# Two tokens of Q and K in a partition, transposed on VectorE as 4-byte pairs

## The chip, the cores and the metric

The kernel runs on one core of one Trainium2 chip. The time is that of the device for one execution, in microseconds (us). Three executions of the kernel before took 408.53, 409.21 and 410.55 us; the median, 409.21, is the time before.

## The reference

Inputs are Q, K and V of shape 8 x 8 x 576 x 64 (batch, head, token, width) and four weight matrices, all fp32. Sliding-window attention comes first: each token attends to itself and the 63 tokens before it.

```
scores = q @ k.T / sqrt(64)
scores = where(0 <= pos_q - pos_k < 64, scores, -1e9)
attn   = exp(scores - max) / (sum + 1e-9)
x      = attn @ v                # heads side by side: 4608 tokens x 512
out    = ((x @ w1) * (x @ w2)) @ w3 @ w_out      # 512 -> 1024 -> 1024 -> 512
```

The output is 4608 x 512 in fp32.

## The kernel before

The kernel works in fp16 with fp32 sums. At the start it folds w3 and w_out into one matrix (`fold_t`, `fold_mm`), so the second half of the network is two matrix products, `ffn_ab` (line 374) and `ffn_o` (line 392).

**Loads.** `load_qk` brings Q or K of one batch into a tile of 128 partitions with two DMAs from GpSimd's queue, which also convert to fp16. A partition holds 18 consecutive tokens of one head, for each of two heads: partition 32 j + p holds tokens 18 p to 18 p + 17 of heads 2 j and 2 j + 1. Each DMA moves one head of each pair as one contiguous piece of 2304 bytes (in SBUF) for each partition. `load_v` brings V in blocks of 128 tokens, in pieces of 128 bytes.

**Transposition.** `transposes(b, which, hh)` is one VectorE instruction (line 211) for one head of each pair. It transposes blocks of 32 x 32 elements inside each group of 32 partitions, so that the 64 components of a head lie on 32 partitions, in two halves c = 0 and c = 1. The tile is ordered (half, token). Blocks are read as 32 consecutive elements; on the write side the fastest index is p, the partition of origin, and tokens p and p + 1 of one block lie 18 elements apart. There are four such instructions for each batch: K and Q, each for hh = 0 and 1.

**Scores.** `scores(n)` takes one of three segments of a batch. It issues 32 matmuls (line 249) with 32 contracted rows, four groups of partitions side by side, and adds the halves c = 0 and c = 1. `weigh` applies the exponential on ScalarE (line 259) and two masks on GpSimd (lines 267 and 269).

**Values.** `values(d)` multiplies probabilities with V (line 312; line 296 in the first two batches), takes the logarithm of the sums and an exponential on ScalarE, and VectorE multiplies (lines 321 and 322, or 304) into the ring `xT`. `ffn_ab` then ends with a VectorE product (line 380) and `ffn_o` with a VectorE copy (line 394) and a store by the SP queue.

**Order.** The order is written out by hand (`manual_schedule`). The first two batches (`SHORT = 2`) are straight-line code. From tick 24 on a batch is twelve ticks, and a list of FFN pieces with due times calls `tick(u)` between them. `late` says which extra steps a tick r of a batch issues, with the batch they are for:

```
late = {0: [("load", 2, "k")], 1: [("t", 1, "k", 0), ("load", 2, "q")], 2: [("v", 1, 0, 2)],
        3: [("t", 1, "q", 0), ("v", 1, 3)], 5: [("t", 1, "k", 1), ("v", 1, 4, 5)], 7: [("t", 1, "q", 1)],
        8: [("copy", 1, 4)], 9: [("copy", 1, 1)]}
```

So K of batch b + 2 is loaded at tick 0 of batch b, and the transpositions of batch b + 1 stand at ticks 1, 3, 5 and 7. Each engine works through its own queue in this order. Score tiles and value tiles come from one pool with two buffers (`ps_a`); FFN tiles from another with four (`ps_f`). The tiles of loaded Q and K have two buffers each.

Of the kernel before, what the change touches and what calls it, by code (L numbers as in the profile page):

```python
# [9 lines left out]
FP16 = mybir.dt.float16  # L10
I32 = mybir.dt.int32
# [4 lines left out]
P = 128  # L16
# [128 lines left out]
def kernel(  # L145
# [11 lines left out]
    nc = tc.nc  # L157
    B, H, S, D = q.shape
# [4 lines left out]
    NJ = H // 2  # L163
    TI = 18
# [5 lines left out]
    SHORT = 2  # L170
# [11 lines left out]
    sb = fast.enter_context(tc.tile_pool(name="sb", bufs=2))  # L182
# [13 lines left out]

    t16s, kTs, qTs = {}, {}, {}

    def load_qk(b, which):
        src = k if which == "k" else q  # L200
        t = sb.tile([P, 2, TI * D], FP16, name=which + "16", bufs=2)
        for hh in range(2):
            nc.gpsimd.dma_start(out=t[:, hh], in_=src[b, hh:H:2].rearrange("j (p r) d -> j p (r d)", r=TI))
        t16s[which, b] = t

    def transposes(b, which, hh):

        dst = kTs if which == "k" else qTs
        if hh == 0:
            dst[b] = sb.tile([P, 2, 2, S], FP16, name=which + "T")  # L210
        nc.vector.transpose(dst[b][:, hh].rearrange("q c (p i) -> q i c p", i=TI), t16s[which, b][:, hh].rearrange(  # L211
            "p (i c e) -> p i c e", c=2, e=32))

    def v_heads(b):
        return v16s[b % 2].rearrange("p c j (a e) -> p c (j a) e", a=2)[:, :, :, 0:D]
# [19 lines left out]
    def scores(n):  # L235

        b, si = divmod(n, 3)
        kT, qT = kTs[b], qTs[b]
        seg = SEGS[si]
        w = sum(blk[2] for blk in seg)  # L240
        s_ps = [ps_a.tile([P, 2, 512], FP32, name="a_ps") for _ in range(2)]
        c0 = 0
        for (k0, q0, m, _) in seg:
            for a in range(2):
                for c in range(2):
                    for j in range(NJ):
                        part = slice(32 * j, 32 * j + 32)
                        o0 = 256 * a + c0
                        nc.tensor.matmul(s_ps[j // 2][:, j % 2, o0:o0 + m], kT[part, a, c, k0:k0 + P],  # L249
                                         qT[part, a, c, q0:q0 + m], start=(c == 0), stop=(c == 1),  # L250
                                         skip_group_check=True)
            c0 += m
        for jp in range(2):
            weigh(2 * n + jp, s_ps[jp].rearrange("k j (a n) -> k j a n", a=2)[:, :, :, 0:w], si, w)

    def weigh(d, s_ps, si, w):

        pt = sb.tile([P, 2, 2, 256], FP16, name="pt", bufs=6)
        nc.scalar.activation(pt[:, :, :, 0:w], s_ps, AF.Exp, bias=-SHIFT, scale=scale)  # L259

        rows = pt.rearrange("k j a n -> k (j a) n")
        for (lo, nb, n, off, step) in MASKS[si]:
            sl = rows[:, :, lo:lo + nb * n]
            pat = [[0, 4], [step, nb], [1, n]]
            if nb == 1:
                pat = [[0, 4], [1, n]]
            nc.gpsimd.affine_select(out=sl, in_=sl, pattern=pat, compare_op=ALU.is_ge,  # L267
                                    fill=0.0, base=off, channel_multiplier=-1)
            nc.gpsimd.affine_select(out=sl, in_=sl, pattern=[[-s, m] for s, m in pat], compare_op=ALU.is_ge,  # L269
                                    fill=0.0, base=63 - off, channel_multiplier=1)  # L270
        probs[d] = pt
# [62 lines left out]
    def event(b, kind, ahead, *a):  # L334
        if b + ahead >= B:
            return
        do = {"load": load_qk, "t": transposes, "v": load_v, "copy": copy_v}[kind]
        do(b + ahead, *a)
# [3 lines left out]
    def tick(u):  # L342

        b, r = divmod(u, 12)
        n, m = divmod(u, 4)
        if m == 0 and n < NS:
            scores(n)
        if m in (1, 2) and 6 < n <= NS:
            values(2 * n - 3 + m)
        for e in late.get(r, []):  # L350
            event(b, *e)
        if m == 3 and 6 < n <= NS:
            keep_sums(n - 1)
# [4 lines left out]
    def ffn_ab(g, fc, nf=1, lo=0, hi=GT):  # L358

        if g not in abs_:  # L360
            abs_[g] = sb.tile([P, 8, GT], FP16, name="ab", bufs=3)
        ab = abs_[g]
        n = hi - lo
        a_ps = ps_f.tile([P, GT], FP32, name="f_ps")
        b_ps = ps_f.tile([P, GT], FP32, name="f_ps")
        x0 = (g * GT + lo) % RING
        cuts = [(0, n)] if x0 + n <= RING else [(0, RING - x0), (RING - x0, n)]
        for w, d in ((w1_sb, a_ps), (w2_sb, b_ps)):
            first = True
            for f in range(nf):  # L370
                for dc in range(4):
                    for c0, c1 in cuts:
                        xc = (x0 + c0) % RING
                        nc.tensor.matmul(d[:, f * n + c0:f * n + c1], w[:, dc, (fc + f) * P:(fc + f + 1) * P],  # L374
                                         xT[:, dc, xc:xc + c1 - c0], start=first, stop=(dc == 3),
                                         skip_group_check=True)
                        first = False
        a_sb = sb.tile([P, GT], FP32, name="a_sb", bufs=3)
        act_cp(a_sb[:, 0:nf * n], a_ps[:, 0:nf * n])  # L379
        nc.vector.tensor_tensor(ab[:, fc:fc + nf, lo:hi], b_ps[:, 0:nf * n].rearrange("p (f n) -> p f n", f=nf),  # L380
                                a_sb[:, 0:nf * n].rearrange("p (f n) -> p f n", f=nf), ALU.mult)
# [92 lines left out]
    def fold_step(fc):  # L474
        if fc + 1 < 8:
            w3Ts[fc + 1] = fold_t(fc + 1)
        fold_mm(fc, w3Ts.pop(fc), act_cp if fc % 4 == 3 else dve_cp)

    load_qk(0, "k")
    load_qk(0, "q")  # L480
    load_wo()
    load_w3(0)
# [3 lines left out]
    for hh in range(2):  # L486
        transposes(0, "k", hh)
        transposes(0, "q", hh)
    keep_busy(30)
    load_v(0, 0, 2, 3)  # L490
    load_w3(2)
    load_w3(3)
    scores(0)
    keep_busy(15)
    scores(1)
    keep_busy(15)
    w3Ts[0] = fold_t(0)
# [69 lines left out]
    for g in range(1, NG):  # L567
        part = [lambda g=g, fc=fc: ffn_ab(g, fc) for fc in range(8)] + \
# [60 lines left out]
```

## Time and profile before

| | |
|---|---|
| median of three runs | 409.21 us (408.53 to 410.55) |
| the profiled execution | 407.49 us |
| its span | 405.8 us |
| TensorE busy, mean granted clock | 291.7 us, 0.852 |
| VectorE busy | 300.1 us |
| ScalarE busy | 149.7 us |
| GpSimd busy | 169.0 us |
| packets on DMA queue 0 (GpSimd's) | 58640 |

The profile is one execution on the chip. In it PE is TensorE, DVE is VectorE, ACT is ScalarE, POOL is GpSimd, SP is the engine that issues the stores; L211 is line 211 of the kernel. The granted clock is the share of full speed that TensorE was given: 1.00 is 2.4 GHz, 0.50 is 1.2 GHz. The span begins with the first recorded instruction and ends with the last; the execution's own time is 1.7 us longer.

### The profile page before, as it was taken

The numbers are of one execution on the slowest core, as the hardware profiler recorded it, in microseconds if no ns is written. First come the engines' busy times: TensorE is split into PE (matmuls) and PEld (weight loads), VectorE is DVE, ScalarE is ACT, GpSimd is POOL, SyncE is SP. The second block draws the span as 40 slices with busy tenths as digits, with TensorE's granted clock in tenths as the row PEclk, the third lists the DMA queues.
The fourth block names the chain that finished last, engine by engine and source line by source line (L and its number), as shares of the span: only waits on it lengthen the run. The fifth ranks groups of instructions, "written<-read, shape, count | busy, mean of one in ns | idle before, by whom it ended". The sixth has DMA issues, their size and how long they took to land.

```text
span 405.8 us, 6273 instructions
## 1 busy us (share of the span) xinstructions
PE 291.7 (72%) x2474; PEld 153.8 (38%) x2474; DVE 300.1 (74%) x267; ACT 149.7 (37%) x256; POOL 169.0 (42%) x218
## 2 busy tenths in 40 slices
PE   8008895747067454987679567978696779999995
PEld 8006452223033212443234233855342335455442
DVE  2892756976956399779977997598969896655542
ACT  1003162125023602364426433524464337764220
POOL 6307943118046852186127704535424533540300
PEclk9757999569668855996889887989899789999999
DMA  5990499911409990129312980299206410020203
GB/s 61 203 188 17 40 165 160 144 15 32 48 28 104 121 128 0 54 69 138 22 52 62 133 38 27 80 124 52 80 28 39 46 55 29 26 80 1 106 1 107
DMA packets 64097, 29.47 MB, mean 73 GB/s; under 512 B 51088, under 2 KB 54416, under 8 KB 64064
## 3 DMA queue, kind: packets, MB, share of 16 engines
q0 software_dynamic: 58640, 19.45, 51.3%
q1 hardware_dynamic: 5280, 9.46, 6.6%
q8 instruction: 20, 0.33, 0.4%
q14 instruction: 13, 0.11, 0.1%
q10 hardware_dynamic: 144, 0.13, 0.1%
HBM read 38.80 MB, written 9.44 MB: 119 GB/s over the span
## 4 chain that ended last, share of the span: by engine, by line
PE 40%; DVE 26%; issue 16%; DMA 10%; POOL 6%; ACT 1%; DVEq 0%; POOLq 0%
PE f_ps L374 22%; PE f_ps L392 11%; DVE qT L211 10%; DVE kT L211 9%; DMA k<-in_k_dram 7%; PE a_ps L312 4%; DMA q<-in_q_dram 3%; DVE ab L380 3%; PE a_ps L249 2%; POOL pt L269 2%; POOL pt L267 2%; DVE xT L322 2%; DVE xT L321 1%; DVE t2k L394 1%; POOL v L223 1%
## 5 line engine op out<-in xcount | busy, mean ns | idle before, releaser
L374 PE MATMUL f_ps<-xT,w_sb 128*128 128x512 f16 (+1 forms) x640 | 151.5, 392 | 30.1 <-DVE ab L380 23.8
L267 POOL TENSOR_SCALAR_AFFINE_SELECT pt<-pt 128x512 f16<-128x512 f16 (+1 forms) x64 | 52.0, 813 | 169.8 <-ACT pt L259 169.8
L374 PEld LDWEIGHTS <-w_sb 128*128 128x128 f16 x640 | 64.3, 104 | 99.3 <-issue 52.4
L211 DVE STREAM_TRANSPOSE kT<-k 128x1152 f16<-128x1152 f16 x16 | 81.9, 5119 | 16.4 <-DMA k<-in_k_dram 16.1
L259 ACT ACTIVATE pt<-a_ps 128x1024 f16<-128x1024 f32 (+1 forms) x48 | 43.1, 950 | 118.3 <-PE a_ps L249 118.3
L211 DVE STREAM_TRANSPOSE qT<-q 128x1152 f16<-128x1152 f16 x16 | 82.1, 5134 | 0.1
L392 PE MATMUL f_ps<-wc_sb,ab 128*128 128x512 f16 (+1 forms) x296 | 75.9, 411 | 7.6 <-DVE ab L380 7.6
L380 DVE TENSOR_TENSOR ab<-f_ps,a_sb 128x512 f16<-128x512 f32 x72 | 51.4, 723 | 32.9 <-PE f_ps L374 18.4
L379 ACT COPY a_sb<-f_ps 128x512 f32<-128x512 f32 x72 | 41.8, 581 | 62.6 <-PE f_ps L374 62.6
L249 PE MATMUL a_ps<-qT,kT 32*128 32x128 f16 (+1 forms) x768 | 19.2, 234 | 63.2 <-DVE xT L322 29.0
L269 POOL TENSOR_SCALAR_AFFINE_SELECT pt<-pt 128x512 f16<-128x512 f16 (+1 forms) x64 | 51.9, 811 | 4.4
L392 PEld LDWEIGHTS <-ab 128*128 128x128 f16 x296 | 29.7, 105 | 44.3 <-issue 10.3
L223 POOL DMA_DIRECT2D v<-in_v_dram x40 | 34.1, 856 | 19.5 <-DMA k<-in_k_dram 17.4
L249 PEld LDWEIGHTS <-kT 32*128 32x128 f16 x768 | 13.7, 103 | 74.4 <-issue 44.2
L394 DVE COPY t2k<-f_ps 128x512 f32<-128x512 f32 (+1 forms) x36 | 24.8, 693 | 13.1 <-PE f_ps L392 12.4
L321 DVE TENSOR_TENSOR xT<-a_ps,r 64x384 f16<-64x384 f32 x36 | 19.6, 546 | 19.0 <-ACT r L320 19.0
L318 ACT ACTIVATE ln_s<-a_ps 64x384 f32<-64x384 f32 x36 | 17.5, 487 | 40.1 <-PE a_ps L312 40.0
L312 PEld LDWEIGHTS <-v 128*128 128x128 f16 x288 | 20.4, 106 | 9.2 <-issue 3.2
L312 PE MATMUL a_ps<-pt,v 128*128 128x128 f16 (+1 forms) x288 | 23.0, 229 | 0.0
L322 DVE TENSOR_TENSOR xT<-a_ps,r 64x384 f16<-64x384 f32 x36 | 20.2, 561 | 0.5
L320 ACT ACTIVATE r<-ln_s 128x384 f32<-128x384 f32 x36 | 18.8, 523 | 1.1
L319 ACT ACTIVATE ln_s<-a_ps 64x384 f32<-64x384 f32 x36 | 17.4, 482 | 0.4
(41 smaller groups left out, 147.5 us busy)
## 6 DMA issues: line engine op xcount, KB each, us to landing
out_dram<-t2k SPq DMA_DIRECT2D x35, 256.0 KB
k<-in_k_dram POOLq DMA_DIRECT2D x16, 288.0 KB, 11.4
q<-in_q_dram POOLq DMA_DIRECT2D x16, 288.0 KB, 12.1
v<-in_v_dram POOLq DMA_DIRECT2D x32, 128.0 KB, 11.1
w_sb<-in_moe_w_dram POOLq DMA_DIRECT2D x4, 512.0 KB, 12.2
ab<-in_moe_w_out_dram POOLq DMA_DIRECT2D x1, 1024.0 KB, 15.7
ab<-in_moe_w_dram POOLq DMA_DIRECT2D x2, 512.0 KB, 18.2
xT<-in_moe_w_dram POOLq DMA_DIRECT2D x2, 512.0 KB, 14.7
```

What stands on the lines that cost most here:

```text
L211: nc.vector.transpose(dst[b][:, hh].rearrange("q c (p i) -> q i c p", i=TI), t16s[which, b][:, hh].rearrange("p (i c e) -> p i c e", c=2, ...
L223: nc.gpsimd.dma_start(out=vh[lo:P, c], in_=v[b, :, s0:s0 + P - lo, :].rearrange("h s d -> s h d"))
L249: nc.tensor.matmul(s_ps[j // 2][:, j % 2, o0:o0 + m], kT[part, a, c, k0:k0 + P], qT[part, a, c, q0:q0 + m], start=(c == 0), stop=(c == 1), ...
L259: nc.scalar.activation(pt[:, :, :, 0:w], s_ps, AF.Exp, bias=-SHIFT, scale=scale)
L267: nc.gpsimd.affine_select(out=sl, in_=sl, pattern=pat, compare_op=ALU.is_ge, fill=0.0, base=off, channel_multiplier=-1)
L269: nc.gpsimd.affine_select(out=sl, in_=sl, pattern=[[-s, m] for s, m in pat], compare_op=ALU.is_ge, fill=0.0, base=63 - off, channel_multip ...
L312: nc.tensor.matmul(o_ps[:, jj, o0:o0 + n], v16[:, si * 2 + bi, j0 + jj, a * D:a * D + P], pt[:, jj, a, c0:c0 + n], start=first, stop=(bi = ...
L374: nc.tensor.matmul(d[:, f * n + c0:f * n + c1], w[:, dc, (fc + f) * P:(fc + f + 1) * P], xT[:, dc, xc:xc + c1 - c0], start=first, stop=(dc ...
L379: act_cp(a_sb[:, 0:nf * n], a_ps[:, 0:nf * n])
L380: nc.vector.tensor_tensor(ab[:, fc:fc + nf, lo:hi], b_ps[:, 0:nf * n].rearrange("p (f n) -> p f n", f=nf), a_sb[:, 0:nf * n].rearrange("p ...
L392: nc.tensor.matmul(o_ps[:, 0:c1 - c0], ab[:, fc, t * P:t * P + P], wc_sb[:, fc, c0:c1], start=(fc == 0), stop=(fc == 7))
L394: cp(o_sb[:, c0:c1], o_ps[:, 0:c1 - c0])
```

## The change

A partition holds runs of r consecutive tokens instead of 18: runs of nine in batches 0 and 1, runs of two in batches 2 to 7. A run of two has nine repeats in a partition, a run of nine has two. `load_qk` issues one DMA for each pair of heads (32 partitions, both heads) instead of one for each member of the pairs (128 partitions): four DMAs instead of two, with pieces of 1152 bytes in SBUF (r = 9) or 256 bytes (r = 2).

`transposes` views two neighbouring fp16 components as one 4-byte integer, so an instruction moves 576 elements instead of 1152. The transposed tile is ordered (token, parity): components 2 e and 2 e + 1 of a token lie side by side on partition e, and tokens p and p + 1 of a block lie r elements of 4 bytes apart. The score matmuls contract the even components and then the odd ones (c is now the parity), and read K and Q with a step of two fp16 elements. Nothing else is changed.

```diff
+    def run(b):
+        return 9 if b < SHORT else 2
+
     def load_qk(b, which):
         src = k if which == "k" else q
+        r = run(b)
         t = sb.tile([P, 2, TI * D], FP16, name=which + "16", bufs=2)
-        for hh in range(2):
-            nc.gpsimd.dma_start(out=t[:, hh], in_=src[b, hh:H:2].rearrange("j (p r) d -> j p (r d)", r=TI))
+        for j in range(NJ):
+            nc.gpsimd.dma_start(
+                out=t[32 * j:32 * j + 32].rearrange("p hh (i n) -> p (hh i) n", n=r * D),
+                in_=src[b, 2 * j:2 * j + 2].rearrange("hh (i p r) d -> p (hh i) (r d)", p=32, r=r))
         t16s[which, b] = t
 
     def transposes(b, which, hh):
         dst = kTs if which == "k" else qTs
+        r = run(b)
         if hh == 0:
-            dst[b] = sb.tile([P, 2, 2, S], FP16, name=which + "T")
-        nc.vector.transpose(dst[b][:, hh].rearrange("q c (p i) -> q i c p", i=TI), t16s[which, b][:, hh].rearrange(
-            "p (i c e) -> p i c e", c=2, e=32))
+            dst[b] = sb.tile([P, 2, S, 2], FP16, name=which + "T")
+        nc.vector.transpose(
+            dst[b][:, hh].rearrange("q t c -> q (t c)").bitcast(I32).rearrange("q (i p r) -> q i r p", p=32, r=r),
+            t16s[which, b][:, hh].bitcast(I32).rearrange("p (i r e) -> p i r e", r=r, e=32))
...
-                        nc.tensor.matmul(s_ps[j // 2][:, j % 2, o0:o0 + m], kT[part, a, c, k0:k0 + P],
-                                         qT[part, a, c, q0:q0 + m], start=(c == 0), stop=(c == 1),
+                        nc.tensor.matmul(s_ps[j // 2][:, j % 2, o0:o0 + m], kT[part, a, k0:k0 + P, c],
+                                         qT[part, a, q0:q0 + m, c], start=(c == 0), stop=(c == 1),
```

## Rows read from the trace of the kernel before

**Rows 1.** The page, busy us (share of the span) and instructions of each engine.

```profile
PE 291.7 (72%) x2474; PEld 153.8 (38%) x2474; DVE 300.1 (74%) x267; ACT 149.7 (37%) x256; POOL 169.0 (42%) x218
```

**Rows 2.** The page, the chain that ended last: shares by line.

```profile
PE f_ps L374 22%; PE f_ps L392 11%; DVE qT L211 10%; DVE kT L211 9%; DMA k<-in_k_dram 7%; PE a_ps L312 4%; DMA q<-in_q_dram 3%; DVE ab L380 3%; PE a_ps L249 2%; POOL pt L269 2%; POOL pt L267 2%; DVE xT L322 2%; DVE xT L321 1%; DVE t2k L394 1%; POOL v L223 1%
```

**Rows 3.** Groups by line and shape: busy us, mean ns | idle before.

```profile
L211 DVE STREAM_TRANSPOSE qT<-q 128x1152 f16<-128x1152 f16 x16 | 82.1, 5134 | 0.1
L211 DVE STREAM_TRANSPOSE kT<-k 128x1152 f16<-128x1152 f16 x16 | 81.9, 5119 | 16.4 <-DMA k<-in_k_dram 16.1
L380 DVE TENSOR_TENSOR ab<-f_ps,a_sb 128x512 f16<-128x512 f32 x72 | 51.4, 723 | 32.9 <-PE f_ps L374 18.4 <-ACT a_sb L379 13.6
...
L223 POOL DMA_DIRECT2D v<-in_v_dram x40 | 34.1, 856 | 19.5 <-DMA k<-in_k_dram 17.4 <-DMA w_sb<-in_moe_w_dram 2.0
...
L394 DVE COPY t2k<-f_ps 128x512 f32<-128x512 f32 x35 | 24.3, 700 | 12.1 <-PE f_ps L392 11.4
...
L203 POOL DMA_DIRECT2D k<-in_k_dram x16 | 11.6, 727 | 1.0 <-issue 0.8
```

**Rows 4.** Windows: length, busy us of each engine, granted clock, DMA share, GB/s.

```profile
65.90:87.60 21.70, 9.54 (x34) 3.12 (x33) 21.70 (x8) 1.80 (x4) 5.20 (x7) 0.68 1.37 120
87.60:125.00 37.40, 19.11 (x232) 9.67 (x232) 27.83 (x20) 12.42 (x20) 18.11 (x23) 0.77 0.26 35
125.00:144.30 19.30, 11.60 (x116) 5.18 (x116) 9.01 (x11) 9.03 (x15) 13.78 (x21) 0.77 0.99 128
144.30:163.00 18.70, 11.39 (x56) 4.15 (x56) 18.58 (x10) 3.02 (x4) 6.67 (x8) 0.51 1.16 49
163.00:350.00 187.00, 147.57 (x1226) 78.04 (x1225) 157.07 (x150) 86.64 (x152) 81.07 (x105) 0.89 0.48 61
350.00:405.80 55.80, 50.86 (x311) 24.92 (x308) 26.81 (x43) 21.36 (x39) 12.33 (x11) 0.99 0.16 58
```

**Rows 5.** Windows, VectorE's busy time with line 211 alone.

```profile
144.30:163.00 18.70, 15.20 (x3) 0.51 1.16 49
163.00:350.00 187.00, 81.97 (x16) 0.89 0.48 61
```

**Rows 6.** The chain that ended last, in order of time: start us, us, what.

```profile
1.61 9.65 DMA k<-in_k_dram
...
31.20 0.66 PE a_ps L249 x21
...
213.98 0.45 PE a_ps L249 x32
...
219.47 1.20 DVE kT L211
```

**Rows 7.** Timeline of VectorE: start us, us, what [idle before, releaser].

```profile
65.90 5.10 DVE L211 STREAM_TRANSPOSE kT<-k 128x1152 f16<-128x1152 f16 x1 [2.37 <-DMA k<-in_k_dram]
...
177.76 5.12 DVE L211 STREAM_TRANSPOSE kT<-k 128x1152 f16<-128x1152 f16 x1
```

**Rows 8.** Timeline of TensorE, near 185 us.

```profile
184.69 1.03 PE L249 MATMUL a_ps<-qT,kT 32*128 32x128 f16 x30 [3.91 <-DVE xT L322]
```

**Rows 9.** Windows, a stretch without transpositions; columns as in rows 4.

```profile
163.40:180.60 17.20, 17.16 (x134) 8.71 (x133) 11.92 (x17) 9.80 (x19) 7.03 (x13) 1.00 0.20 64
```

**Rows 10.** Waits (us in total, times, longest), then GpSimd's timeline at 11.55.

```profile
PE a_ps L249 <- DVE xT L322: 29.0, 8, 5.3
POOL v L223 <- DMA k<-in_k_dram: 17.4, 4, 9.0
...
11.55 0.88 POOL L223 DMA_DIRECT2D v<-in_v_dram  x1 [3.76 <-DMA k<-in_k_dram]
```

**Rows 11.** Line 203, the Q and K loads, from issue to landing.

```profile
DMA to landing us min/median/max: 9.4/11.9/16.8
```

**Rows 12.** DMA packets from 43 to 45.5 us (V) and from 50 to 54 (weights).

```profile
DMA packets 1514, 0.19 MB, mean 76 GB/s; under 512 B 1514, under 2 KB 1514, under 8 KB 1514
...
DMA packets 788, 0.79 MB, mean 198 GB/s; under 512 B 16, under 2 KB 788, under 8 KB 788
```

## The prediction

> **What bounds the kernel now.** I read five views in this order. The page's busy times first: VectorE is busy 74% of the span, TensorE 72% [rows 1]. Neither is full, so the two must wait for each other. Then the shares of the chain of waits: the reader should see line 211, the transposition, with 10% (Q) and 9% (K) of the span, the largest piece that is not a TensorE matmul, and DMA of K and Q with 10% [rows 2]. Then the groups by line: 32 transpositions of 5.12 to 5.13 us, 164.0 us of VectorE's 300.1 [rows 3].
>
> Then the windows, which tell the stages apart [rows 4]. From 65.9 to 87.6 us VectorE is busy all the time and TensorE 9.5 of 21.7. From 144.3 to 163 VectorE is busy 18.6 of 18.7, 15.2 of it transpositions [rows 5], and TensorE runs at a granted clock of 0.51, nearly all at the lower level (1.2 GHz). From 163 to 350 TensorE is busy 147.6 of 187 at a mean clock of 0.89. From 350 on there are no transpositions, and it is busy 50.9 of 55.8 at 0.99.
>
> Last the time order inside a batch. A transposition at 177.76 takes 5.12 us in VectorE's queue; the scores at 184.69 have waited 3.91 us for the division at line 322 that stands behind it, since score tiles and value tiles share two PSUM buffers [rows 7, 8]. That wait adds up to 29.0 us [rows 10]. In the 17.2 us before, which hold no transposition, TensorE is busy 17.16 us at clock 1.00 [rows 9]. So between 65.9 and 350 the kernel is bound by VectorE's transpositions and by the clock that TensorE loses in the idle time they cause; without them it is bound by TensorE.
>
> **A transposition after the change.** It moves 576 elements of 4 bytes instead of 1152 of 2. The trace shows no transposition of 4-byte elements and none with another write step, so I bound it. Upper end but one: the same time per element, 5.12 x 576/1152 = 2.56 us. Upper end: the same time per byte, 5.12 us. Lower end: what VectorE needs per element where it writes a dense row of 4-byte elements, 0.700 us for 512 (line 394), so 0.79 us [rows 3]. Today each transposition costs 4.44 ns per element against 1.37 there, and what sets it apart in the code is the write: its fastest index steps by 18 elements of 2 bytes, 36 bytes. With runs of nine (batches 0 and 1) the new step is 9 x 4 = 36 bytes, the same, so I take 2.56 us. With runs of two (batches 2 to 7) it is 8 bytes, nearer to the dense 4 than to 36, so I take 0.79 us.
>
> The Trainium skill ("SBUF — State Buffer", Specifications (TRN2)) says that SBUF has lines of 16 bytes and gives full bandwidth only with two or more accesses to a line. By that rule the runs of two would reach the lower end, and the runs of nine stay slow. The trace agrees only in that today's 36-byte step is three times dearer per element than a dense row; no run here shows the 8-byte step.
>
> **The loads.** Each load becomes four DMAs instead of two, so GpSimd issues 64 instead of 32. At 0.727 us for a K issue today and 0.856 for a V issue, which has eight times as many pieces to a partition [rows 3], I take 0.75: 48 us against 22, so 26 us more on GpSimd. GpSimd is busy 169 us of 406 [rows 1] and mostly waits for exponentials; I cost this at nothing except between 87.6 and 125, where its 18.1 us [rows 4] come to some 21.
>
> For runs of two, K and Q of a batch are 8 x 576 = 4608 pieces of 256 bytes in SBUF. The V pieces of 128 bytes are the nearest row: 1514 of them went in a stretch of 2.5 us [rows 12], so 4608 take 7.6 us if the number counts. The weights went at 198 GB/s [rows 12]; by bytes, 4608 x 256 bytes = 1.18 MB take 6.0 us, as they would in today's pieces. A batch lasts 41.7 us now (177.76 to 219.47, rows 6 and 7), and its loads are issued a batch ahead. So this is hidden, at 0 us; it would begin to cost only at several times that.
>
> **The score matmuls** read K and Q with a step of two. The least is no change, the most that reading takes twice as long: a score set is 0.45 us [rows 6], 24 sets, 10.8 us. Step and value stay within the same few bytes, and the weight loads overlap; I take 0.
>
> **Stage by stage**, against the profiled execution (407.49 us, span 405.8):
>
> - Start, to 31.2 us. The first K half lands 9.65 us after its issue at 1.61, then four transpositions follow, and the scores run at 31.20 [rows 6]. K must now land whole before the first one. I keep 11.3 us for that: the same bytes in twice the DMAs. Then 11.3 + 4 x 2.56 = 21.5, gain 9.7. Ends: 14 (0.79 each) and 31 (5.12 each). The weights are issued behind the loads and so later; the fold that uses them follows two score sets, which I count as cover; without it the stage ends as much later as they land.
> - 31.2 to 65.9. VectorE idles 2.37 us for K of batch 1 [rows 7]. All before it moves forward with the scores, GpSimd's masks and so the loads too: gain 2.4.
> - 65.9 to 87.6. Four transpositions alternate with four products of 0.72 us [rows 3, 4], all VectorE. New: 4 x (2.56 + 0.72 to 0.87) = 13.1 to 13.7, gain 8.
> - 87.6 to 125. Four transpositions, now of two-token runs: 4 x 4.33 = 17.3 less on VectorE. Next late is GpSimd with its 21 us of masks and issues. 37.4 becomes 23.4, gain 14.
> - 125 to 144.3. TensorE is busy 11.6 of 19.3 [rows 4]; the rest is K of batch 3 landing, then its transposition. Landing takes 9.4 to 16.8 us today [rows 11]. The load is issued as far ahead of its use as before, so part of the wait can stay: of the 7.7 us I take 6.
> - 144.3 to 163. VectorE's 18.6 lose 15.2 and get 3 x 0.79 back: 5.8. TensorE's 11.4 at clock 0.51 come to about 6 at 1.00. I take 9.2 for the chain between them, gain 9.5.
> - 163 to 350. Idle: 187 - 147.6 = 39.4 us. A mean clock of 0.89 means the lower level for 22% of the time, 41 us; at the same busy share that is 32 us of work, which takes 16 at 2.4 GHz. So TensorE's work is 147.6 - 16 = 131 us. VectorE then holds 157.1 - 82.0 + 16 x 0.79 = 88 us, ScalarE 87, GpSimd 81 + 9: all below. I add 8 us for starts and clock falls that stay: 139, gain 48.
> - 350 to the end: nothing.
>
> Sum: 9.7 + 2.4 + 8 + 14 + 6 + 9.5 + 48 = 97.6, so 407.5 - 97.6 = 309.9. The median shown is 409.21, 1.7 above the profiled run: 312 us.
>
> **Rivals.**
>
> *Two-token transpositions keep the time per element (2.56 us).* For: the trace has only that row for this operation. Against: the step. Each one of the 16 after 163 us costs (39.4 + 16)/16 = 3.5 us now, so TensorE hides 1.6 of 5.12; of 2.56 it would see 1 us, or 16 with what I left as rest, 8 more than taken. With 4 x 1.77 = 7 before 125, 2 before 144 and 3 x 1.77 = 5 before 163 that is 22: 334 us.
>
> *GpSimd stops at its own DMAs.* It waited 17.4 us, four times, for K loads to land before a V issue; the first was at 11.55, its ninth DMA [rows 10]. If only eight may be under way, that is what it waits for. A batch has 13 now instead of 9, so K's four and Q's four fill that depth, and V's issue waits behind K, and the masks behind V. Against: a K landing takes 9.4 to 16.8 us, but two ticks of 41.7/12 = 3.5 us and the mask's lag of four ticks lie between. If half a landing (6 us) shows in each of six batches: 36 us, 348 us.
>
> *The change buys nothing*: a transposition of pairs takes 5.12 us by the byte, and the time stays at 409, give or take 2.
>
> *The small pieces decide, slower.* Place: the K and Q loads of batches 2 to 7, nine times the pieces of today, 288 for each of the 16 engines a batch. What speaks for it: V at 76 GB/s against 198 for the weights [rows 12]. V and the stores need about 9 us a batch (three such V stretches of 2.5 us and a little for the stores). The start's 20 us are still gained. So the kernel gets slower once 288 t + 9 passes 41.7 + 20/6 = 45, at t = 125 ns a piece and engine. From the V stretch t is 2.5 x 16/1514 = 26 ns, which speaks against. At 140 ns a batch takes 49.3 us: 409 + 6 x 7.6 - 20 = 435 us. The Trainium skill ("DMA: Bandwidth & Descriptors", Specifications) states that below 512 bytes a transfer falls short of line rate because of a read-modify-write. By that rule these 256-byte pieces would be slow where today's 2304-byte ones are not; the trace agrees in direction, 76 against 198 GB/s, not in a size that decides.
>
> **Chances.** Forecast 0.62, own range 296 to 328; 2.56 us at every transposition 0.20; GpSimd's stops 0.07; nothing gained 0.05; slower through the pieces 0.06. The low end takes 0.79 us also for the runs of nine (7 us at the start, up to 7 before 87.6) and less rest after 163: 294. The high end holds the first rival with score reads at twice the time, 334 + 11, and the edge of the second: 348. About two in ten lie outside. A measurement of this kernel tells about 0.5% from no change. Faster 0.89, same 0.04, slower 0.07.
>
> **What would show it.** Right: line 211 has two durations, near 0.8 and near 2.6 us; VectorE's busy time falls to about 176 us (300 - 164 + 8 x 2.56 + 24 x 0.79 = 175.5); the scores' first run comes near 21 us; the granted clock is near 1.00 from 163 on; TensorE leads the chain and line 211 all but leaves it. Wrong: one duration at 2.6 or 5; score matmuls longer than 0.45 us a set; DMA of K or Q or a mask ending TensorE's waits; a K landing that takes longer than 17 us.

## The result, and the profile after

The changed kernel takes 291.4 us (median of 4 runs, 289.86 to 292.08) against 409.88 (408.53 to 411.10): ratio 0.7105, 95% interval 0.7064 to 0.7145. The forecast was 312 us with a range of 294 to 348, so the time lies below the range. The direction and the bound were right; the gain was under-sized by 20 us. Single runs over 1.5% above the fastest of their kernel, at a lower granted clock (two of pairs18's four, one of r3's, one of the kernel before's), are left out of the times below.

The page of the changed kernel, for [rows 1] and [rows 2]: busy us (share of the span) of each engine, its queue of K, Q and V loads (packets, MB, share of 16 engines), then the shares of the chain that ended last, by engine.

```profile
span 288.1 us, 6332 instructions
PE 260.2 (90%) x2474; PEld 144.1 (50%) x2474; DVE 171.6 (60%) x267; ACT 149.7 (52%) x256; POOL 187.7 (65%) x250
...
q0 software_dynamic: 72464, 19.41, 75.1%
...
PE 48%; POOL 21%; DMA 19%; DVE 5%; issue 4%; ACT 2%; DVEq 0%; POOLq 0%
```

VectorE fell from 300.1 to 171.6 us, TensorE is busy 90% of the span, and the chain belongs to TensorE, GpSimd and transfers: VectorE has 5% of it where the transposition alone had 19%.

Groups by line, for [rows 3]: busy us, mean ns of one, idle before.

```profile
L383 PE MATMUL f_ps<-xT,w_sb 128*128 128x512 f16 (+1 forms) x640 | 133.5, 361 | 2.4 <-DVE xT L313 2.4
...
L232 POOL DMA_DIRECT2D v<-in_v_dram x40 | 34.0, 857 | 1.1 <-DMA k<-in_k_dram 0.4
...
L208 POOL DMA_DIRECT2D q<-in_q_dram x32 | 20.1, 635 | 6.7 <-DMA w_sb<-in_moe_w_dram 3.6
...
L208 POOL DMA_DIRECT2D k<-in_k_dram x32 | 20.6, 650 | 5.2 <-DMA w_sb<-in_moe_w_dram 3.0
...
L219 DVE STREAM_TRANSPOSE kT<-k 128x576 int32<-128x576 int32 x16 | 14.2, 889 | 8.8 <-DMA k<-in_k_dram 8.5
```

The mean of 889 ns mixes two shapes of run. Line 219's K transpositions in 0 to 16, 16 to 60 and 60 to 200 us (ns, least/median/most) part them: 1.2 us for runs of nine in batches 0 and 1, 0.78 us for runs of two.

```profile
L219 DVE STREAM_TRANSPOSE kT<-k x2: 1180/1202/1225, 8.8 to 12.8; 128x576 int32<-128x576 int32 x2
L219 DVE STREAM_TRANSPOSE kT<-k x2: 1206/1208/1209, 47.9 to 51.4; 128x576 int32<-128x576 int32 x2
L219 DVE STREAM_TRANSPOSE kT<-k x10: 769/780/800, 64.7 to 184.0; 128x576 int32<-128x576 int32 x10
```

The windows below are cut at the events that stood in [rows 4] or near them: first whole score run, first K transposition of batch 1, score sets 3, 6, 9 and 23.

```profile
0.00:15.10 15.10, 9.03 (x138) 8.87 (x139) 7.10 (x5) 1.28 (x1) 11.65 (x22) 0.98 0.90 135
15.10:47.90 32.80, 30.16 (x355) 18.58 (x355) 16.30 (x25) 12.99 (x21) 26.50 (x36) 0.90 1.23 177
47.90:55.75 7.85, 7.85 (x37) 3.42 (x36) 7.08 (x9) 2.93 (x5) 3.01 (x5) 1.00 2.63 153
55.75:79.85 24.10, 18.14 (x249) 9.34 (x250) 12.82 (x23) 12.91 (x21) 20.17 (x27) 1.00 0.97 106
79.85:111.12 31.27, 25.25 (x218) 11.72 (x218) 16.53 (x27) 15.14 (x25) 26.06 (x35) 0.95 1.34 109
111.12:164.70 53.58, 51.29 (x484) 26.37 (x484) 38.27 (x63) 36.75 (x64) 44.66 (x58) 1.00 1.01 109
164.70:239.07 74.37, 74.37 (x738) 44.15 (x742) 51.02 (x83) 50.41 (x88) 47.67 (x62) 1.00 0.57 78
239.07:288.10 49.03, 44.15 (x267) 21.66 (x266) 22.52 (x37) 17.33 (x31) 7.99 (x7) 1.00 0.16 56
```

From 164.70 to 239.07 TensorE is never idle and its granted clock is 1.00 (2.4 GHz). Before, the mean from 163 to 350 was 0.89 with 39 us idle. Between score sets 3 and 9, from 55.75 to 111.12, 6 us of idle time are left in each of two windows; the start has another 6 and the end 5.

By the same events the stages compare so (us; the forecast's gain is that of the step in the prediction, its steps from 87.6 on taken together):

| stage ends with | before | after | gain | forecast |
|---|---|---|---|---|
| first whole score run | 31.20 | 15.10 | 16.1 | 9.7 |
| K transposition of batch 1 begins | 65.90 | 47.90 | 1.9 | 2.4 |
| score set 3 | 87.61 | 55.75 | 13.9 | 8 |
| score set 9 | 172.20 | 111.12 | 29.2 | |
| score set 23 | 356.73 | 239.07 | 56.6 | |
| from score set 3 to 23 | 269.1 | 183.3 | 85.8 | 77.5 |
| end of the span | 405.8 | 288.1 | 0.0 | 0 |

The gains sum to 117.7 us against 97.6.

### The profile page after: what moved, and what is told of

Its sections match the earlier page's. It is cut to its first block, busy times and chain, and to the rows that moved or that the text cites. A ratio compares the mean times of both kernels' runs of the same rounds, so it can differ in the third digit from the quotient of the medians.

```text
span 288.1 us, 6332 instructions
## 1 busy us (share of the span) xinstructions
PE 260.2 (90%) x2474; PEld 144.1 (50%) x2474; DVE 171.6 (60%) x267; ACT 149.7 (52%) x256; POOL 187.7 (65%) x250
## 3 DMA queue, kind: packets, MB, share of 16 engines
q0 software_dynamic: 72464, 19.41, 75.1%
## 4 chain that ended last, share of the span: by engine, by line
PE 48%; POOL 21%; DMA 19%; DVE 5%; issue 4%; ACT 2%; DVEq 0%; POOLq 0%
PE f_ps L383 26%; PE f_ps L401 15%; DMA v<-in_v_dram 14%; POOL pt L278 6%; POOL pt L276 6%; PE a_ps L321 3%; POOL v L232 3%; PE a_ps L258 3%; POOL q L208 3%; DMA w_sb<-in_moe_w_dram 3%; POOL k L208 2%; DMA q<-in_q_dram 2%; ACT pt L268 1%; DVE t2k L403 1%; DVE xT L331 1%
## 5 line engine op out<-in xcount | busy, mean ns | idle before, releaser
L383 PE MATMUL f_ps<-xT,w_sb 128*128 128x512 f16 (+1 forms) x640 | 133.5, 361 | 2.4 <-DVE xT L313 2.4
L383 PEld LDWEIGHTS <-w_sb 128*128 128x128 f16 x640 | 60.5, 98 | 59.3 <-issue 5.8
L389 DVE TENSOR_TENSOR ab<-f_ps,a_sb 128x512 f16<-128x512 f32 x72 | 49.1, 687 | 37.5 <-ACT a_sb L388 20.5
L401 PE MATMUL f_ps<-wc_sb,ab 128*128 128x512 f16 (+1 forms) x296 | 66.4, 374 | 2.9 <-DVE ab L389 2.9
L401 PEld LDWEIGHTS <-ab 128*128 128x128 f16 x296 | 27.5, 98 | 32.5 <-DVE ab L389 3.9
L330 DVE TENSOR_TENSOR xT<-a_ps,r 64x384 f16<-64x384 f32 x36 | 19.6, 545 | 16.1 <-ACT r L329 16.0
L327 ACT ACTIVATE ln_s<-a_ps 64x384 f32<-64x384 f32 x36 | 17.5, 487 | 16.1 <-PE a_ps L321 15.8
L208 POOL DMA_DIRECT2D q<-in_q_dram x32 | 20.1, 635 | 6.7 <-DMA w_sb<-in_moe_w_dram 3.6
L258 PE MATMUL a_ps<-qT,kT 32*128 32x128 f16 (+1 forms) x768 | 16.6, 216 | 8.4 <-DVE qT L219 4.5
L208 POOL DMA_DIRECT2D k<-in_k_dram x32 | 20.6, 650 | 5.2 <-DMA w_sb<-in_moe_w_dram 3.0
L219 DVE STREAM_TRANSPOSE kT<-k 128x576 int32<-128x576 int32 x16 | 14.2, 889 | 8.8 <-DMA k<-in_k_dram 8.5
L329 ACT ACTIVATE r<-ln_s 128x384 f32<-128x384 f32 x36 | 18.8, 523 | 1.1
## 6 DMA issues: line engine op xcount, KB each, us to landing
ab<-in_moe_w_dram POOLq DMA_DIRECT2D x2, 512.0 KB, 13.9
xT<-in_moe_w_dram POOLq DMA_DIRECT2D x2, 512.0 KB, 17.1
```

Source lines behind the costliest of these rows:

```text
L208: nc.gpsimd.dma_start(out=t[32 * j:32 * j + 32].rearrange("p hh (i n) -> p (hh i) n", n=r * D), in_=src[b, 2 * j:2 * j + 2].rearrange("hh ...
L401: nc.tensor.matmul(o_ps[:, 0:c1 - c0], ab[:, fc, t * P:t * P + P], wc_sb[:, fc, c0:c1], start=(fc == 0), stop=(fc == 7))
```

## The experiments

Eleven kernels ran. The first question was what makes a transposition of pairs cheap: the write's step, or the width of an element. The other was what the new loads do.

**micro**: the two kinds of transposition at six write steps each.

```
for r in (1, 2, 3, 6, 9, 18):      # pairs: 576 elements of 4 bytes
    nc.vector.transpose(dst.bitcast(I32).rearrange("q (i p r) -> q i r p", p=32, r=r), ...)
for r in (1, 2, 4, 6, 9, 18):      # fp16: 1152 elements of 2 bytes
    nc.vector.transpose(dst.rearrange("q (i p r) -> q i r p", p=32, r=r), ...)
```

> This kernel leaves out the whole computation: it transposes a constant tile four times for each of twelve cases and runs 128 matmuls of 32 contracted rows for each of four read steps. Cases: pairs (576 elements of 4 bytes) written with runs of 1, 2, 3, 6, 9, 18, that is steps of 4, 8, 12, 24, 36, 72 bytes; single fp16 (1152 elements of 2 bytes) with runs of 1, 2, 4, 6, 9, 18, steps of 2 to 36 bytes. Theory S (the write step sets the price, as the prediction had it): pairs 0.8 us up to 8 bytes, more with each step, 1.2 at 36, and single fp16 elements are cheap too at small steps, about 1.3 to 1.6 us at 2 to 8 bytes, 5.1 only at 36. Theory E (the width of the element sets it): pairs 0.8 to 1.2 at every step, fp16 near 5.1 at every step. Score-like matmuls: the prediction's value is no change between steps 1 and 2 (0.45 us for 32); its upper end is twice that at step 2.

The rows show three stretches of pairs and three of fp16, with least/median/most ns. In each stretch instructions of two runs alternate: 1 and 2, 3 and 6, 9 and 18 for the pairs; 1 and 2, 4 and 6, 9 and 18 for fp16. A row may hold one instruction of the stretch before.

```profile
L167 DVE STREAM_TRANSPOSE pair_r<-src x8: 720/740/743, 6.8 to 11.4; 128x576 int32<-128x576 int32 x8
L167 DVE STREAM_TRANSPOSE pair_r<-src x9: 743/964/1200, 11.4 to 18.3; 128x576 int32<-128x576 int32 x9
L167 DVE STREAM_TRANSPOSE pair_r<-src x9: 1200/1270/1309, 18.3 to 26.7; 128x576 int32<-128x576 int32 x9
L172 DVE STREAM_TRANSPOSE half_r<-src x8: 1384/1456/1534, 27.8 to 36.8; 128x1152 f16<-128x1152 f16 x8
L172 DVE STREAM_TRANSPOSE half_r<-src x9: 1528/2883/4070, 36.8 to 59.8; 128x1152 f16<-128x1152 f16 x9
L172 DVE STREAM_TRANSPOSE half_r<-src x9: 4068/5340/5433, 59.8 to 98.3; 128x1152 f16<-128x1152 f16 x9
```

The means by run, in us:

| write step, bytes | 2 | 4 | 8 | 12 | 18 | 24 | 36 | 72 |
|---|---|---|---|---|---|---|---|---|
| pairs, 576 x 4 bytes | | 0.73 | 0.74 | 0.94 | | 1.18 | 1.25 | 1.29 |
| fp16, 1152 x 2 bytes | 1.40 | 1.52 | 2.86 | 4.07 | 5.41 | | 5.34 | |

Both matter. At small steps either kind takes 1.2 to 1.3 ns an element, so a pair saves half by count. At wide steps a 2-byte element takes 4.6 to 4.7 ns and a 4-byte one 2.2 ns. The old price, 5.12 us, becomes 1.25 at the same 36 bytes: half the elements at half the price each.

The score-like matmuls of this kernel (32 contracted rows, 128 columns) took 214 ns on the average with a read step of one and 214 ns with a step of two.

**pairs18**: the pairs alone, with the old loads and 18 tokens a partition (a step of 72 bytes).

```
-        return 9 if b < SHORT else 2
+        return TI
-        for j in range(NJ):
-            nc.gpsimd.dma_start(out=t[32 * j:32 * j + 32]..., in_=src[b, 2 * j:2 * j + 2]...)
+        for hh in range(2):
+            nc.gpsimd.dma_start(out=t[:, hh], in_=src[b, hh:H:2].rearrange("j (p r) d -> j p (r d)", r=TI))
```

> Pairs alone: transposition of 4-byte pairs and score reads with a step of two, with the old loads (18 tokens a partition, two DMAs) and so a write step of 72 bytes. Theory: what the change bought is VectorE's time, so whatever the 72-byte step costs between 1.2 and 2.6 us, most of the 118 us comes: 300 to 335 us. Rival: the new loads carry a good part (K and Q landing sooner, spread over all DMA engines): 350 us or more with the pairs alone.

304.2 us (two runs, 303.99 and 304.33) against 410.32: 106.2 us of the gain without new loads or short runs, as the first theory had it. A transposition takes 1.25 us, near micro's 1.29 for 72 bytes. VectorE now waits for K, as its transposition group on the page shows (18.8 us before the K transpositions):

```profile
L217 DVE STREAM_TRANSPOSE kT<-k 128x576 int32<-128x576 int32 x16 | 20.0, 1253 | 19.1 <-DMA k<-in_k_dram 18.8
```

The landing of its K and Q loads, from issue:

```profile
DMA to landing us min/median/max: 9.8/12.5/18.2
```

Three pieces of its chain that ended last (start us, us), all K in transfer:

```profile
37.17 18.24 DMA k<-in_k_dram
58.22 15.74 DMA k<-in_k_dram
88.12 11.32 DMA k<-in_k_dram
```

**loads_by_pair**: the old kernel with four loads by pair of heads instead of two by parity, the runs of 18 kept.

```
-        for hh in range(2):
-            nc.gpsimd.dma_start(out=t[:, hh], in_=src[b, hh:H:2].rearrange("j (p r) d -> j p (r d)", r=TI))
+        for j in range(NJ):
+            nc.gpsimd.dma_start(out=t[32 * j:32 * j + 32],
+                                in_=src[b, 2 * j:2 * j + 2].rearrange("hh (p r) d -> p hh (r d)", r=TI))
```

> The loads alone: the kernel before, with its runs of 18 tokens and its fp16 transpositions, but each load as four DMAs of one pair of heads (32 partitions, both heads) instead of two DMAs of 128 partitions. Theory: VectorE still bounds; only the first K and Q land sooner (K 8.8 instead of 11.3 us, as in the changed kernel) and the two exposed waits for K get shorter: 395 to 407 us. Rival: loads carry a third of the gain: 370 us or less.

397.22 us, ratio 0.9696 (0.9627 to 0.9765): 13 us less. The transposition still takes 5.13 us, so the 13 us are the loads'. Its landing:

```profile
DMA to landing us min/median/max: 3.0/5.4/12.6
```

Its window from 4 to 8 us, when K and Q are in flight (the last number is GB/s):

```profile
4.00:8.00 4.00, 4.00 (x55) 4.00 (x53) 0.23 (x1) 0.00 (x0) 4.00 (x8) 1.00 1.04 167
```

and the same window of the kernel before:

```profile
4.00:8.00 4.00, 4.00 (x62) 4.00 (x60) 0.23 (x1) 0.00 (x0) 3.79 (x5) 1.00 0.73 82
```

The same K and Q move at twice the rate, and the median landing falls from 11.9 us [rows 11] to 5.4, though for DMAs of half the size (144 KB instead of 288).

**pairs18_by_pair**: both of these together, still with runs of 18, in the changed kernel:

```
-        return 9 if b < SHORT else 2
+        return TI
```

> Pairs with runs of 18 tokens, as in the run of the pairs alone (306.6 us), but loaded by pair of heads as in the changed kernel: pieces of 2304 bytes, write step 72 bytes. Theory: the 15 us between the pairs alone and the whole change are the shape of the loads (a DMA over four pairs of heads occupies only part of the DMA engines, so K lands 15 to 18 us after its issue), not the runs: 289 to 295 us, and K lands some 6 us after its issue. Rival: the runs matter through step or piece: 298 us or more.

289.93 us, ratio 0.7084 (0.7039 to 0.7128), the changed kernel's time within the intervals. The group on its page, and then the landing:

```profile
L219 DVE STREAM_TRANSPOSE kT<-k 128x576 int32<-128x576 int32 x16 | 20.1, 1256 | 8.3 <-DMA k<-in_k_dram 8.0
```

```profile
DMA to landing us min/median/max: 2.9/5.4/12.3
```

VectorE's wait for K falls from 18.8 us in pairs18 to 8.0, and the time by 14.2. The same events in the three profiled executions (us) show where:

| stage ends with | pairs18 | pairs18_by_pair | as changed |
|---|---|---|---|
| first whole score run | 19.36 | 15.04 | 15.10 |
| score set 3 | 63.23 | 55.50 | 55.75 |
| score set 9 | 121.41 | 110.36 | 111.12 |
| score set 23 | 253.82 | 238.88 | 239.07 |
| end of the span | 302.6 | 287.6 | 288.1 |

So the change is two things, pairs and loads by pair of heads (106.2 and 13.1 us each alone, about 120 together), and the short runs add nothing: 0.78 us instead of 1.25 is VectorE's time, and VectorE seldom ends the waits now.

**no_pairs**: the changed kernel's loads and runs, with two fp16 transpositions a head pair instead of one of pairs.

```
-            dst[b] = sb.tile([P, 2, S, 2], FP16, name=which + "T")
+            dst[b] = sb.tile([P, 2, 2, S], FP16, name=which + "T")
...
+        for c in range(2):
+            nc.vector.transpose(dst[b][:, hh, c].rearrange("q (i p r) -> q i r p", p=32, r=r), src[:, :, :, c])
```

> The changed kernel without the pairs: its loads and runs (nine, then two), but fp16 elements transposed by two VectorE instructions for each head (one for each half c), 576 elements of 2 bytes each, write steps 18 and 4 bytes, and score reads with a step of one. Theory S: the 4-byte step is cheap, two instructions of about 0.8 us, 1.6 instead of 0.78: 293 to 310 us. Theory E: 2-byte elements cost 4.44 ns each at any step, so 5.1 us as before: 385 to 410 us.

325.02 us in one run, between what the two theories gave (293 to 310, and 385 to 410). Line 221's K transpositions before 60 us (all of nine) and from 60 us on, two of them to one of pairs:

```profile
L221 DVE STREAM_TRANSPOSE kT<-k x4: 2724/2868/2878, 8.7 to 21.1; 128x576 f16<-128x576 f16 x4
...
L221 DVE STREAM_TRANSPOSE kT<-k x28: 754/817/2898, 60.9 to 246.1; 128x576 f16<-128x576 f16 x28
```

Runs of nine cost 2 x 2.87 us, no less than before (the 2898 of the second row is one of batch 1's); runs of two cost 2 x 0.82 = 1.6 us instead of 5.12. Without pairs the short runs are worth a great deal: 397.22 us in loads_by_pair, 325.02 here. With pairs the dear case costs only 1.25, which is why they aren't.

**r9_all, r2_all, r3, r1**: run lengths in the changed kernel: `return 9`; `return 2`; `return 9 if b < SHORT else 3`; `return 9 if b < SHORT else 1`.

> The changed kernel with runs of nine in all batches: write step 36 bytes, so 1.2 us for each of the 24 later transpositions instead of 0.78, and pieces of 1152 bytes instead of 256. Theory: after the pairs VectorE has slack wherever TensorE is fully busy, and the 15 us by which the pairs alone stay behind (306.6 against 291.4) are the loads', not the step's: 288 to 295 us. Rival: the step matters, and the first rival of the prediction was right in kind: 10 us of VectorE time come back as 300 us or more.

> Runs of two in the first two batches too: transpositions 0.78 instead of 1.21 there, but the first K and Q come in 4608 pieces of 256 bytes instead of 1024 of 1152. Theory: the start is bound by the landing, not by the transpositions; the pieces cost about what they save, 0.4 us for each transposition: 289 to 294 us. Rival (the pieces are slow): K lands some 3 us later or more at the start and again in batch 1: 295 us or more.

> Runs of three instead of two in batches 2 to 7: write step 12 bytes, 0.94 us by the measurement of single transpositions instead of 0.74; 3072 pieces of 384 bytes for K and Q of a batch instead of 4608 of 256. Theory: neither the step nor the pieces decide, same within 1%: 289 to 293 us. Rival (the pieces load the DMA engines): V lands sooner and it is 2 to 4 us faster.

> Runs of one in batches 2 to 7: twice the suspected cost of the pieces, 9216 of 128 bytes for K and Q of a batch (15.2 us at the rate of the V pieces) against 4608 of 256; the write step falls to 4 bytes, 0.73 us. Theory: a batch lasts some 27 us and its other transfers take some 9, so the pieces still fit; they only make V land later: 291 to 300 us. Rival (the prediction's slower case, small pieces decide): the loads of a batch outlast it, 310 us or more.

| run | us | ratio, 95% interval | K transposition, mean us | packets of the load queue |
|---|---|---|---|---|
| r9_all | 291.94 | 0.7128 (0.7080 to 0.7175) | 1.22 | 50960 |
| r3 | 289.36 | 0.7052 (0.6995 to 0.7109) | 1.04 | 63248 |
| as changed | 291.40 | 0.7105 (0.7064 to 0.7145) | 0.89 | 72464 |
| r2_all | 292.44 | 0.7140 (0.7069 to 0.7211) | 0.78 | 79632 |
| r1 | 293.85 | 0.7201 (0.7135 to 0.7267) | 0.88 | 100112 |

The first four can't be told apart. r1, with 128-byte pieces (9216 for K and Q of a batch), stands some 2.5 us above the changed kernel. Its four runs are all slower than the changed kernel's four, but the intervals overlap, so the size of the loss isn't settled. The times of its packets add up to nearly the whole span of sixteen engines:

```profile
span 292.1 us, 6332 instructions
...
q0 software_dynamic: 100112, 19.41, 99.1%
```

This doesn't show that the queue is full: packet times overlap, as the share of 2.63 in a window above shows. In the changed kernel a packet of that queue takes 0.751 x 288.1 x 16 / 72464 = 48 ns on the average, overlap counted double.

**v_first**: in the changed kernel's late batches, V's loads go ahead of K's and Q's.

```
-    late = {0: [("load", 2, "k")], 1: [("t", 1, "k", 0), ("load", 2, "q")], 2: [("v", 1, 0, 2)],
-            3: [("t", 1, "q", 0), ("v", 1, 3)], 5: [("t", 1, "k", 1), ("v", 1, 4, 5)], 7: [("t", 1, "q", 1)],
+    late = {0: [("v", 1, 0, 2)], 1: [("t", 1, "k", 0), ("v", 1, 3)], 3: [("t", 1, "q", 0), ("v", 1, 4, 5)],
+            4: [("load", 2, "k")], 5: [("t", 1, "k", 1)], 6: [("load", 2, "q")], 7: [("t", 1, "q", 1)],
```

> The changed kernel with another order of the late loads: V of the next batch at ticks 0, 1 and 3 and K and Q of the batch after at ticks 4 and 6, instead of K, Q, then V. Theory: what TensorE still loses between 80 and 165 us is the copy of V on VectorE that waits for V behind eight K and Q DMAs (7.19 us at 103 us in the trace) and GpSimd's own waits; with V ahead those go: 4 to 7 us faster, 284 to 288 us. Rival: DMA throughput or GpSimd's time is the limit there, and the order only moves the wait: 290 to 293 us.

284.49 us (283.96 to 284.99), ratio 0.6954 (0.6912 to 0.6995), ahead of both kernels, as the theory had it. The changed kernel's timeline shows a wait that goes. On VectorE a copy of V waits 7.19 us, and a product (line 389) stands behind it; on TensorE the matmul that needs a product waits 2.69 us (start us, us, what [idle before, releaser]):

```profile
103.37 0.43 DVE L236 COPY v<-v 64x512 f16<-64x512 f16 x1 [7.19 <-DMA v<-in_v_dram]
103.83 0.69 DVE L389 TENSOR_TENSOR ab<-f_ps,a_sb 128x512 f16<-128x512 f32 x1
...
104.57 0.39 PE L401 MATMUL f_ps<-wc_sb,ab 128*128 128x512 f16 x1 [2.69 <-DVE ab L389]
```

In v_first's timeline the copy has no such wait, and on TensorE the longest wait for a product between 70 and 120 us is 0.20:

```profile
96.36 0.72 DVE L236 COPY v<-v 64x512 f16<-64x512 f16 x1
...
91.40 1.02 PE L383 MATMUL f_ps<-xT,w_sb 128*128 128x512 f16 x4 [0.20 <-DVE ab L389]
```

Its busy times on the page:

```profile
PE 257.5 (91%) x2474; PEld 143.2 (51%) x2474; DVE 173.6 (62%) x267; ACT 149.6 (53%) x256; POOL 187.2 (66%) x250
```

Of the 5.9 us between the two spans (288.1 to 282.2), 2.7 are TensorE's busy time at a mean clock of 0.993 instead of 0.981, the rest idle time. The stage in which the copy waited, from score set 6 to 9, has 4.4 of the 5.9: it takes 26.90 us (79.52 to 106.42) instead of 31.27.

**v_first_r9**: the same order, with `return 9`.

> The order with V ahead (284.5 us) together with runs of nine in all batches: fewer pieces, a dearer transposition (1.2 us). Theory: once V is ahead, neither the pieces nor 0.4 us a transposition are late next: 283 to 286 us, no better. Rival: the pieces still cost: 279 to 282 us.

287.94 us, ratio 0.7035 (0.6982 to 0.7088): a miss, slower than either guess (283 to 286, and 279 to 282). That fewer pieces would help once V comes first isn't borne out. Of the 3.7 us between the two spans (285.9 and 282.2), 2.5 are lost between score sets 3 and 6, and in the values of batch 1 (line 305) TensorE waits 5.6 us for GpSimd's masks instead of 2.0. Why the masks come later wasn't settled.

## What of the prediction was right, and which steps failed

**The bound.** Right. Between 65.9 and 350 us the kernel was bound by the transpositions and the clock lost around them, and then by TensorE: busy 74.37 of 74.37 us at 1.00. pairs18, which changes only the transposition's form and the score reads that follow from it, takes 106.2 us off.

**Runs of two: 0.79 us taken, 0.78 measured.** The dense row of 4-byte elements was the right neighbour for an 8-byte step; micro has 0.73 and 0.74 us at 4 and 8 bytes.

**Runs of nine: the first step that failed.** The prediction took "the same time per element" for the same 36 bytes, 2.56 us. Measured: 1.18 to 1.23. The step in bytes was the same, the width of what is written was not, and the price per element halves with it. Eight such transpositions stand on the path, four at the start and four from 47.9 us on: 8 x 1.35 = 10.8 us that the sum was short. By itself this would have made the forecast 301 us, still inside the range. VectorE's busy time of 171.6 us lies near the 176 foretold partly by luck: its transpositions take 28.3 us where 39.4 were counted, and the rest of its work, some of which had overlapped with transpositions, counts for 7 us more.

The Trainium skill ("SBUF — State Buffer", Specifications (TRN2)) asks for two accesses to a 16-byte line. For pairs the trace agrees: 0.74 us at 8 bytes, 0.94 at 12, 1.18 and more from 24 on. For 2-byte elements it does not: a step of 8 bytes also has two to a line and takes 2.86 us against 1.40. The measurement decides, and by it the rule gave no price for runs of nine.

**K's first landing.** 11.3 us were kept; K lands whole at 8.84, since the loads by pair of heads moved 169 GB/s from 4 to 8 us where the old ones moved 82. That is 2.5 us gained beyond the forecast, of which a wait for Q takes 1.73 back (start us, us, [idle before]):

```profile
8.84 1.23 DVE L219 STREAM_TRANSPOSE kT<-k 128x576 int32<-128x576 int32 x1 [4.61 <-DMA k<-in_k_dram]
11.80 1.20 DVE L219 STREAM_TRANSPOSE qT<-q 128x576 int32<-128x576 int32 x1 [1.73 <-DMA q<-in_q_dram]
```

**The loads at nothing: the second step that failed.** The prediction saw only more DMAs with the same bytes and priced the rearranged load at nothing. It costs GpSimd 40.7 us of issues (48 taken), and gives 13 us alone and 14 beside the pairs. By the profiled executions pairs18, with the old loads, gains 405.8 - 302.6 = 103.2 us where the sum had 97.6; the new loads add 14.5. Of these, 4.3 come before the first whole score run, 3.2 from there to score set 3, and 7.3 up to score set 23; the tail is 0.3 longer. So most of what the sum was short is theirs. This overlaps with the 10.8 us above: behind the shorter transpositions VectorE waits 18.8 us for K and 3.6 for Q in pairs18 (16.1 and none before), and the new loads take much of that away. That the sum let all waits for K but a little go was right by luck.

The Trainium skill ("DMA: Bandwidth & Descriptors", Why a DMA increments its semaphore by 16 and not by 1) says that a DMA is spread over the largest number of engines, up to 16, that divides the slowest dimension of both sides. The old load's slowest source dimension is the four head pairs, the new one's is 32 partitions: four engines against sixteen. The trace agrees in rate and landing, and in its packets (queue 0 on the pages of pairs18 and then pairs18_by_pair: packets, MB, share of 16 engines):

```profile
q0 software_dynamic: 58640, 19.45, 77.0%
q0 software_dynamic: 46864, 19.41, 60.2%
```

Both kernels move K and Q in the same 4096 pieces of 2304 bytes, and the second has 32 DMAs more, yet 11776 packets fewer. Counted by size in the traces, the first has 13584 packets of 4 bytes; the second has 1808, which is 16 for each of its 113 DMAs. Beyond 16 a DMA the first has 12288, which is 12 x 32 for each of its 32 DMAs of K and Q. That is what one would see if such a DMA put its 128 pieces on four engines, 32 on each, and gave each of the other twelve 32 small packets. The pieces in flight fit. In pairs18 they are 4.1, 8.4, 12.7 and 15.8 on the average from 3.5 to 4.5, 5 to 6, 6.5 to 7 and 7.5 to 9 us, as its first four DMAs come under way one after the other; in pairs18_by_pair they are 16.3, 15.8, 17.1 and 17.1. The trace doesn't name the engines and no run varied their number alone, so four against sixteen is inferred from these counts and the shapes.

**The 8 us of rest after 163.** Nearly all gone: from score set 9 to 23 the gain is 56.6 us where 48 was taken for nearly the same stretch, and TensorE idles 2.3 of the 127.95 us that are left. In pairs18, with the old loads, it idles 4.9 there. From 87.6 to score set 9 the gain of 29.2 us meets the 29.5 of three steps (14, 6, 9.5).

So the excess of 20.1 us is 6.4 at the start, 5.9 in the stage of batch 1's transpositions, 8.3 from score set 3 on, less 0.5 between the first two. The range's low end, 294, had runs of nine at 0.79 us and less rest, but nothing for the loads.

**What was costed at nothing.** The score reads with a step of two are free: by the groups by form, the 128-column matmuls take 215 ns in 164 to 240 us of the changed kernel, and 215 and 218 ns in two stretches at clock 1.00 before. The pieces of 256 bytes are hidden, as r9_all and r2_all show. The tail is the same: 49.03 us from the last scores on, 49.07 before.

**The rivals.** Two-token transpositions at 2.56 us: no, 0.78. Nothing gained: no. Small pieces: with pieces of half the size r1 loses some 2.5 us, if the difference is real; 48 ns a packet is far from the 125 at which they would have decided. GpSimd's stops: there are some, but not at the price. Waits of K and Q issues by line (us in total, times, longest):

```profile
POOL q L208 <- DMA w_sb<-in_moe_w_dram: 3.6, 2, 2.0
POOL k L208 <- DMA w_sb<-in_moe_w_dram: 3.0, 2, 1.7
...
POOL q L208 <- DMA v<-in_v_dram: 2.1, 3, 1.3
...
POOL k L208 <- DMA v<-in_v_dram: 0.7, 1, 0.7
```

These come to 9.4 us, not to the 36 on the path that the rival asked for. By GpSimd's timeline 7.6 of them stand before 55.75, at the loads of batches 1 and 2, and one of 1.26 us at 84.19. From 55.75 to 79.85 TensorE's 6 idle us are waits for a mask (line 278, 3.2 us) and for a division (line 313, 2.8). GpSimd's first mask there stands behind the last of these issues until 58.11, so the stops may have a part in it; how much wasn't tried.

## What to carry to other kernels

Where VectorE transposes 2-byte data into strided rows, move pairs as 4-byte elements and let the matmul read with a step of two. Read the shape of a load as well as its bytes: a rearranged load of the same bytes gave 13 to 14 us. Once TensorE is full, the order of loads that others queue behind is the next place to look; moving V first gave 7 us.

## What the hardware showed that wasn't expected

A strided transposition's price goes with the width of the element as well as with the step: 4.6 ns a 2-byte element, 2.2 ns a 4-byte one at 36 bytes. A step of 4 bytes costs 2-byte elements little (1.52 us against 1.40), one of 8 doubles them. K and Q loads cut by pair of heads moved 167 GB/s where loads by parity of heads moved 82, and a DMA whose outer dimension was four pairs of heads came with 384 four-byte packets beside its 128 pieces, beyond the 16 of every DMA. Pieces of 128 bytes cost the kernel at most a few us against 256 (293.85 and 291.40 us, intervals overlapping).
